# Small float32 units for short expert tails in a one-core attention and expert kernel

## The chip, the cores and the metric

The kernel runs on one core of one Trainium2 chip. The metric is device time in microseconds of one execution: 991.23 us is the median of three runs of the kernel before (988.27 to 992.65). Times inside an execution are in us from the first instruction of the profiled one.

## The reference, cut to what matters

Three stages follow each other: windowed attention over 4 x 768 tokens, a mixture of experts in which each token goes to one expert, and a dense layer with a rational activation. The change touches the second.

```python
N, D, E, F = (3072, 512, 8, 1024)
logits = x @ w_gate + modality_bias[modality_id]
e_idx = np.argmax(logits, axis=1)
...
for e in range(E):
    mask = e_idx == e
    if not mask.any():
        continue
    h = np.maximum(x[mask] @ w1[e], 0.0)
    out[mask] = gate_w[mask, None] * (h @ w2[e])
```

## The kernel before, in words

Attention works through 24 tiles of 128 tokens and writes each tile's output x to a buffer xd in HBM. `Router` then counts the tokens of each expert and cuts every expert's list into units of 128 tokens: the expert that is most frequent in the first 16 tiles comes first, the others follow by index, and the last unit of each expert may be partly empty. `second` (line 521) holds this arithmetic as a list of small VectorE operations that are issued by hand between TensorE's first products: the number of units of each expert (c), where each expert's units begin (off) and end (end), and each token's slot (slot, from T, lines 548 to 565). From the slots follow, by products with one-hot matrices, the token numbers of each unit (src_u, line 589), their places in the output buffer yd (pos_u) and the gate values (gate_s). `slots` (line 637) writes three flags per unit: is its expert another than that of the unit before, which expert is it, and is the unit used.

`Experts` does the units. `gather` (line 709) fetches the x of a unit by an indirect DMA that GpSimd (POOL) issues, into one of three buffers xg. `prep_x` (line 812) transposes it on TensorE and splits it into a high and a low float32r part. `mm1` (line 823) is three products, in 24 matmuls of 512 columns: x high and x low with w1 high, x high with w1 low. `relu` follows on ScalarE, `prep_h` (line 746) transposes and splits h in two halves, `mm2` (line 755) has again 24 matmuls, and `out` (line 765) scales by the gate on ScalarE and scatters the rows to yd by an indirect DMA from POOL. The raw weights of an expert, 2 MB for w1 and 2 MB for w2, are fetched by `load_w` (line 725) in four DMAs on SyncE's (SP's) queue, and split by `split_w` (line 738) on ScalarE and VectorE, both only where the flag says that the expert changes. SP, ScalarE and VectorE each read the flags and branch.

`moe` (line 841) is the order of the work, written out by hand: iteration i issues mm1 of unit i with the two halves of prep_h of unit i - 1 in between, then relu of unit i, prep_x of unit i + 1, and mm2 of unit i - 1. The weights w1 of unit i + 2 are fetched at the end of iteration i, those of w2 of unit i in its middle. Units 0 to 2 are partly done in `second`, units 3 to 25 in this loop, always; units 26 to 30 lie behind a branch that is taken only if the flag of unit 26 says so. Every engine runs its instructions in this order, and TensorE never goes past an instruction that waits.

`filler` is one step of `converter` (line 958), which turns the int64-coded weights of the third stage into float32r pairs: one DMA into the double buffer wr on SP, casts on ScalarE, five operations on VectorE. The loop calls it twice in an iteration while i < 12 and once after that.

Of the kernel before, what the change touches and what calls it, by code (L numbers as in the profile page):

```python
# [15 lines left out]
U32 = mybir.dt.uint32  # L16
# [266 lines left out]
        rt.second()  # L283


NS = 31
D_M = 512
BIGI = 4096.0
GP = 2048.0
# [3 lines left out]
class Router:  # L293
# [8 lines left out]
    def __init__(self, nc, rk, wk, tp, ident, logits, mod, mbias, pos_u, out_u, ex):  # L302
        self.pos_u, self.out_u, self.ex = pos_u, out_u, ex
        self.nc, self.wk, self.tp, self.ident, self.L = nc, wk, tp, ident, logits
        self.mod, self.mbias, self.src_u, self.flags = mod, mbias, ex.src_u, ex.flags

        def one(shape, dt, name):
            return rk.tile(shape, dt, name=name)

        self.iota = one([P, P], F16, "iota")  # L310
        self.tri = one([P, P], F16, "tri")
        self.ones = one([P, P], F16, "ones")
        self.w8 = one([P, E], F32, "w8")
# [10 lines left out]
        self.s = one([P, 6, E], F32, "s")  # L324
        self.k = one([P, 3], F32, "k")
        self.pidx = one([P, 1], F32, "pidx")
        one([P, 16], F32, "pad_k")
# [14 lines left out]
    def fixed(self):  # L342
        G = self.nc.gpsimd
        G.iota(self.i32, pattern=[[1, P]], base=0, channel_multiplier=0, allow_small_or_imprecise_dtypes=True)
        G.iota(self.w8, pattern=[[-1, E]], base=E, channel_multiplier=0, allow_small_or_imprecise_dtypes=True)

        G.iota(self.tok[:, 0:NT // 2], pattern=[[P, NT // 2]], base=-NT * P // 2, channel_multiplier=1, allow_small_or_imprecise_dtypes=True)
        G.iota(self.tok[:, NT // 2:], pattern=[[P, NT // 2]], base=1, channel_multiplier=1, allow_small_or_imprecise_dtypes=True)
        G.iota(self.pidx, pattern=[[0, 1]], base=0, channel_multiplier=1, allow_small_or_imprecise_dtypes=True)
# [171 lines left out]
    def second(self):  # L521
# [12 lines left out]
        rest = self.first_rest()  # L534
        for f in rest[:2]:
            f()
        c, end, off, hot, lt, other = [self.s[:, i] for i in range(6)]
        hi, slot = self.v[:, 3], self.v[:, 5]
        at2 = self.at2
        S3 = [P, 32, NT]  # L540
        be = self.wk.tile(S3, F16, tag="pt", name="be")
# [4 lines left out]
        for f in (  # L546
            p[0],
            lambda: V.tensor_scalar(out=c, in0=ps[:, NT - n], scalar1=1.0 / P, scalar2=127.0 / 256, op0=ALU.mult, op1=ALU.add),
            p[1],
            lambda: V.tensor_scalar(out=c, in0=c, scalar1=ROUND, scalar2=-ROUND, op0=ALU.add, op1=ALU.add),  # L550
            p[2],
            lambda: V.tensor_tensor_scan(out=end, data0=self.ones[:, 0:E], data1=c, initial=0.0, op0=ALU.mult, op1=ALU.add),
            p[3],
            lambda: V.tensor_tensor(out=hot, in0=hot, in1=c, op=ALU.mult),
            p[4],
            lambda: V.reduce_sum(self.k[:, 2:3], hot, axis=AX.X),
            lambda: V.tensor_tensor(out=off, in0=end, in1=c, op=ALU.subtract),
            lambda: V.scalar_tensor_tensor(out=off, in0=lt, scalar=self.k[:, 2:3], in1=off, op0=ALU.mult, op1=ALU.add),
            lambda: V.tensor_tensor(out=off, in0=off, in1=other, op=ALU.mult),
            lambda: V.tensor_tensor(out=self.T, in0=self.O, in1=off[:, None, :].to_broadcast([P, NT, E]), op=ALU.mult),  # L560
            lambda: V.reduce_sum(slot, self.T, axis=AX.X),
            lambda: V.tensor_tensor(out=s16, in0=slot, in1=hi, op=ALU.add),
            lambda: V.tensor_tensor(out=be, in0=s16[:, None, :].to_broadcast(S3), in1=self.ix, op=ALU.is_equal),
            lambda: V.tensor_tensor(out=bt, in0=be, in1=self.tok[:, None, :].to_broadcast(S3), op=ALU.mult),
            lambda: self.rows(at2, n, NT),
        ):
            f()
# [29 lines left out]
        self.slots(c, end, off, f, cnt)  # L597
        low = ex.prep_x(EARLY)
        ex.relu(1)
        ex.mm2_0(0, 0)  # L600
# [33 lines left out]
        ex.out(1, ex.ys1)  # L634
        ex.load_w(EARLY, ex.w2r, ex.w2v)

    def slots(self, c, end, off, f, cnt):

        V = self.nc.vector
        le = self.wk.tile([P, 32, E], F32, tag="pT", name="le")  # L640
        z, fl = f[:, 2], f[:, 3:6]
        S3 = [P, 32, E]
        V.tensor_tensor(out=end, in0=off, in1=c, op=ALU.add)
        V.tensor_tensor(out=le, in0=end[:, None, :].to_broadcast(S3), in1=self.iota[:, 0:32, None].to_broadcast(S3), op=ALU.is_gt)
        le2 = self.wk.tile([P, 32, E], F32, tag="pT", name="le2")
        V.tensor_tensor(out=le2, in0=off[:, None, :].to_broadcast(S3), in1=self.iota[:, 0:32, None].to_broadcast(S3), op=ALU.is_le)
        V.tensor_tensor(out=le, in0=le, in1=le2, op=ALU.mult)
        V.tensor_tensor(out=le, in0=le, in1=self.w8[:, None, :].to_broadcast(S3), op=ALU.mult)
        V.reduce_sum(z, le, axis=AX.X)
        V.tensor_scalar(out=fl[:, 2, :], in0=z, scalar1=0.0, scalar2=None, op0=ALU.is_gt)  # L650
        V.tensor_scalar(out=fl[:, 1, :], in0=z, scalar1=-1.0, scalar2=float(E), op0=ALU.mult, op1=ALU.add)
        V.tensor_scalar_min(fl[:, 1, :], fl[:, 1, :], float(E - 1))
# [11 lines left out]
class Experts:  # L664


    def __init__(self, nc, tc, ident, xd, yd, w1, w2, src_u, pos_u, out_u, gate_s):
        self.nc, self.tc, self.ident = nc, tc, ident
        self.xd, self.yd, self.src_u, self.pos_u, self.out_u, self.gate_s = xd, yd, src_u, pos_u, out_u, gate_s
        self.w1v = w1.rearrange("e (p k) f -> (e p) (k f)", k=4)  # L670
        self.w2v = w2.rearrange("e (p j) d -> (e p) (j d)", j=8)
        self.hps, self.yps, self.hT = {}, {}, {}
        self.ctx = ExitStack()
        self.sp = self.ctx.enter_context(tc.tile_pool(name="shared", side="right", bufs=1))
# [50 lines left out]
    def load_w(self, s, raw, view):  # L725
        nc = self.nc
        ch = nc.sync.value_load(self.flags[0:1, 0, s:s + 1], min_val=0, max_val=1)
        e = nc.sync.value_load(self.flags[0:1, 1, s:s + 1], min_val=0, max_val=E - 1)
        with self.tc.If(ch == 1):
            self.load(e, raw, view)  # L730

    def split_hi(self, raw, hi, i):
        self.nc.scalar.copy(hi[:, i], raw[:, i])  # L733
# [71 lines left out]
    def relu(self, s):  # L805
        ps = self.hps.pop(s)
        for i in range(2):
            self.nc.scalar.activation(
                self.hs[:, :, i * 64:(i + 1) * 64].rearrange("p j q -> p q j"), ps[i].rearrange("p (q j) -> p q j", j=8), func=AF.Relu,
            )  # L810
# [24 lines left out]
                )  # L835


NM = NT + 2


def moe(nc, tc, ex, filler, rows):
# [2 lines left out]
    w1r, w1h, w1l, w2r, w1v, w2v = ex.w1r, ex.w1h, ex.w1l, ex.w2r, ex.w1v, ex.w2v  # L844
    w2h, w2l = ex.w2h, ex.w2l
    gather, load_w, split_w, mm1, relu, prep_h, mm2, out = ex.gather, ex.load_w, ex.split_w, ex.mm1, ex.relu, ex.prep_h, ex.mm2, ex.out
    for i in range(EARLY + 1, NM + 1):
# [27 lines left out]
        if i == NM:  # L875
            for t in range(4):
                ps = ex.ps.tile([P, 4, P], F32, tag="t", name="yps") if t < 2 else ex.pb[t - 2].rearrange("p (k n) -> p k n", k=4)
                rows.prep(t, w1r[:, t, 0:D_M + 1], ps, rows.h, rows.l)

        if i + 1 < NM:  # L880
            split_w(i + 1, w1r, w1h, w1l)
        if i + 2 < NM:
            load_w(i + 2, w1r, w1v)
        if i == NM:
            ALL = (ET.PE, ET.Activation, ET.DVE, ET.Pool)
# [1 line left out]
            tc.mark_branch_hint_location("more", "LikelyTaken", engines=(ET.PE,))  # L887
        for part in range(2):
            mm2(i - 1, part)
        filler()  # L890
        out(i - 1)
    with tc.If(more == 1, label="more"):  # L892
        for i in range(NM, NS):
            load_w(i, w1r, w1v)
            load_w(i, w2r, w2v)
            split_w(i, w1r, w1h, w1l)
# [357 lines left out]
```

## Time and profile before

| | |
|---|---|
| time of the profiled execution | 991.19 us |
| its span, first to last instruction | 989.4 us |
| TensorE (PE) busy | 958.0 us, 97% |
| VectorE (DVE) busy | 749.6 us, 76% |
| ScalarE (ACT) busy | 594.6 us, 60% |
| GpSimd (POOL) busy | 146.5 us, 15% |
| attention, about | 0 to 107 us |
| router and experts, about | 107 to 447 us |
| third stage, about | 447 to 984 us |

A busy time is the time in which an engine had an instruction in flight. In a timeline a row is a run of instructions of the same kind: its start, how long it took, the engine, the line, what is written and read, the number of instructions, and in brackets the idle time just before it with what ended it. PE's records overlap: the next one starts before the last has ended, so the distance between starts is the price of a row. A plain float32 product leaves two records, a float32r product one. For a DMA, the time to landing runs from its issue to the arrival of its last byte.

### The profile page before, as it was taken

The page shows a single profiled execution, that of the slowest core. Times are in us where ns is not written, and L with a number is a line of the kernel's source. Part 1 is how long each engine was busy: PE and PEld are TensorE (multiplying, and loading weights), DVE is VectorE, ACT ScalarE, POOL GpSimd, SP SyncE. Part 2 cuts the span into 40 slices and gives each one's busy share as a digit, 9 for nine tenths or more (in the row PEclk, how much of TensorE's full clock was granted, in tenths as well). Part 3 has the DMA queues.
Part 4 walks back from the last instruction along what each step waited for, and adds up shares of the span by engine and source line. Part 5 has one row for each costly group of instructions (what it writes and reads, how often), then busy time and mean ns, then how long its engine had stood idle before and what let it go on. Part 6 is the DMA issues. An engine that isn't in the chain of part 4 may idle for free.

```text
span 989.4 us, 16219 instructions
## 1 busy us (share of the span) xinstructions
PE 958.0 (97%) x5825; PEld 780.5 (79%) x5825; DVE 749.6 (76%) x1220; ACT 594.6 (60%) x947; POOL 146.5 (15%) x205
## 2 busy tenths in 40 slices
PE   4998999999899999999999999999999999999997
PEld 3776678888778888887888888888888888888885
DVE  5777664666675553347999989988998998999885
ACT  2554534555575654456777766766676676767673
POOL 5111112111133333220000100100010001001001
PEclk9999999999999999999999999999999999999999
DMA  8999522443686654347120100100010000001001
GB/s 258 364 387 355 201 76 81 128 129 110 230 306 221 232 149 129 124 152 288 34 85 11 43 22 23 43 1 21 23 43 11 22 23 32 21 1 43 1 1 42
DMA packets 37991, 110.41 MB, mean 112 GB/s; under 512 B 6950, under 2 KB 6978, under 8 KB 37892
## 3 DMA queue, kind: packets, MB, share of 16 engines
q1 hardware_dynamic: 27540, 76.43, 23.1%
q0 software_dynamic: 10352, 32.79, 9.3%
q8 instruction: 46, 0.75, 0.3%
q14 instruction: 53, 0.43, 0.1%
HBM read 82.44 MB, written 27.80 MB: 111 GB/s over the span
## 4 chain that ended last, share of the span: by engine, by line
PE 52%; DVE 1%; DMA 1%; ACT 0%; issue 0%; POOLq 0%; SPq 0%; POOL 0%; DVEq 0%
PE a L1126 9%; PE a L1124 9%; PE a L1125 9%; PE h L1067 8%; PE h L1069 8%; PE h L1068 8%; PE yps L952 1%; DMA wo<-wod 1%; DVE gl L1109 0%; DVE u L1099 0%; DVE q L1086 0%; DVE q L1098 0%; DVE q L1097 0%; DVE u L1087 0%; POOLq L1250 0%
## 5 line engine op out<-in xcount | busy, mean ns | idle before, releaser
L1067 PE MATMUL h<-yh,wih 128*128 128x512 f32 x384 | 151.7, 395 | 0.4 <-PEq L892 0.4
L1126 PE MATMUL a<-wo,gl 128*128 128x512 f32 x384 | 149.7, 390 | 1.3 <-DVE gl L1109 1.3
L1124 PE MATMUL a<-wo,gh 128*128 128x512 f32 x384 | 149.5, 389 | 0.7 <-ACT gh L1103 0.7
L1068 PE MATMUL h<-yl,wih 128*128 128x512 f32 x384 | 149.6, 390 | 0.0
L1069 PE MATMUL h<-yh,wil 128*128 128x512 f32 x384 | 149.6, 390 | 0.0
L1125 PE MATMUL a<-wo,gh 128*128 128x512 f32 x384 | 149.4, 389 | 0.0
L832 PE MATMUL pb<-w1h,xs 128*128 128x512 f32 x400 | 104.2, 403 | 2.7 <-ACT w1h L733 2.7
L1079 ACT ACTIVATE s<-h 128x512 f32<-128x512 f32 x96 | 56.6, 590 | 80.2 <-PE h L1069 80.2
L1086 DVE SCALAR_TENSOR_TENSOR q<-s,ab,q 128x512 f32<-128x512 f32 x96 | 71.7, 747 | 27.5 <-ACT q L1080 27.5
L832 PEld LDWEIGHTS pb<-w1h,xs 128*128 128x128 f32 x400 | 74.1, 191 | 18.7 <-ACT w1h L733 3.2
L1103 ACT CAST gh<-u 128x512 fp32r<-128x512 f32 x96 | 59.9, 624 | 46.2 <-DVE u L1099 46.2
L1126 PEld LDWEIGHTS a<-wo,gl 128*128 128x128 f32 x384 | 72.1, 188 | 17.0 <-DVE gl L1109 2.1
L1124 PEld LDWEIGHTS a<-wo,gh 128*128 128x128 f32 x384 | 72.1, 188 | 16.1 <-ACT gh L1103 1.3
L1069 PEld LDWEIGHTS h<-yh,wil 128*128 128x128 f32 x384 | 72.1, 188 | 15.5
L1067 PEld LDWEIGHTS h<-yh,wih 128*128 128x128 f32 x384 | 72.1, 188 | 15.3 <-issue 0.8
L1125 PEld LDWEIGHTS a<-wo,gh 128*128 128x128 f32 x384 | 72.1, 188 | 14.9
L1068 PEld LDWEIGHTS h<-yl,wih 128*128 128x128 f32 x384 | 72.2, 188 | 14.4
L1081 ACT ACTIVATE u<-h,ab 128x512 f32<-128x512 f32 x96 | 74.9, 780 | 0.0
L1099 DVE SCALAR_TENSOR_TENSOR u<-u,ab,q 128x512 f32<-128x512 f32 x96 | 72.2, 752 | 3.4
L1088 DVE SCALAR_TENSOR_TENSOR u<-u,ab,h 128x512 f32<-128x512 f32 x96 | 71.8, 748 | 3.4
L753 DVE TENSOR_TENSOR hl<-hTp,hh 128x512 fp32r<-128x512 f32 x50 | 34.1, 688 | 50.6 <-ACT hh L752 50.4
L1097 DVE SCALAR_TENSOR_TENSOR q<-q,ab,s 128x512 f32<-128x512 f32 x96 | 71.7, 747 | 0.1
(225 smaller groups left out, 1754.1 us busy)
## 6 DMA issues: line engine op xcount, KB each, us to landing
v<-in_v SPq DMA_DIRECT2D x48, 260.0 KB, 5.4
w1r<-in_moe_w SPq DMA_DIRECT2D x16, 512.0 KB, 6.7
w2r<-in_moe_w SPq DMA_DIRECT2D x16, 512.0 KB, 8.7
wr<-in_moe_w_in SPq DMA_DIRECT2D x16, 512.0 KB, 3.7
wr<-in_moe_w_out SPq DMA_DIRECT2D x16, 512.0 KB, 4.4
wod<-wo POOLq DMA_DIRECT2D x32, 256.0 KB, 4.6
wo<-wod SPq DMA_DIRECT2D x16, 512.0 KB, 8.4
k<-in_k SPq DMA_DIRECT2D x48, 168.0 KB, 5.2
```

The source lines that it names most:

```text
L832: self.nc.tensor.matmul(ps[i], lhsT=x[:, kk, :], rhs=w[:, kk, i * 512:(i + 1) * 512], start=(x is h and w is w1h and kk == 0), stop=(w is ...
L1067: nc.tensor.matmul(ps, lhsT=wih[k][:, sl], rhs=h[:, k], start=(k == 0), stop=False)
L1068: nc.tensor.matmul(ps, lhsT=wih[k][:, sl], rhs=l[:, k], start=False, stop=False)
L1069: nc.tensor.matmul(ps, lhsT=wil[k][:, sl], rhs=h[:, k], start=False, stop=(k == NK - 1))
L1081: A.activation(u, ps, func=AF.Identity, scale=a3, bias=a2)
L1086: V.scalar_tensor_tensor(out=q, in0=s, scalar=absb1, in1=q, op0=ALU.mult, op1=ALU.add)
L1088: V.scalar_tensor_tensor(out=u, in0=u, scalar=a1, in1=ps, op0=ALU.add, op1=ALU.mult)
L1097: V.scalar_tensor_tensor(out=q, in0=q, scalar=cb, in1=s, op0=ALU.add, op1=ALU.mult)
L1099: V.scalar_tensor_tensor(out=u, in0=u, scalar=a0, in1=q, op0=ALU.add, op1=ALU.mult)
L1124: nc.tensor.matmul(ps, lhsT=gh[:, sl], rhs=wo[x][:, 0].bitcast(F32R), start=(x == 0), stop=False)
L1125: nc.tensor.matmul(ps, lhsT=gh[:, sl], rhs=wo[x][:, 1].bitcast(F32R), start=False, stop=False)
L1126: nc.tensor.matmul(ps, lhsT=gl[:, sl], rhs=wo[x][:, 0].bitcast(F32R), start=False, stop=(x == NF - 1))
```

## The change

Up to two experts whose last, partly filled unit holds at most 32 tokens lose that unit; a small unit takes its tokens instead. The router finds such tails (sm), takes them out of the count c, and gives the first of them slot 31 and the second slot 30. The static loop has 24 units (NM = NT) and not 26. The first small unit is done in iterations 5 and 6, the second in iterations 7 and 8.

A small unit uses the raw float32 weights, in the buffers w1r and w2r, without any split. Its w1 is fetched at the end of the iteration before, its w2 in the middle of its first iteration, both without a condition. Its 32 rows are gathered into the buffer of the unit whose x has just been used, which also holds its transposed x, its h and its transposed h. mm1_small makes 16 float32 matmuls with 32 stationary columns each; the four that follow each other write four different groups of 32 partitions of one bank of PSUM. mm2_small makes 32 of them in the same way. The gathers of units 8 and 10 move from the start of iterations 6 and 8 to behind the small unit's output. The double calls of filler last while i < 14.

```diff
-NS = 31
+NS = 32
+NN = 31
+SMALL = 2
+SM = 32
...
+            lambda: V.scalar_tensor_tensor(out=sm, in0=c, scalar=float(P), in1=ps[:, NT - n], op0=ALU.mult, op1=ALU.subtract),
+            p[3],
+            lambda: V.tensor_scalar(out=sm, in0=sm, scalar1=float(P - SM), scalar2=None, op0=ALU.is_ge),
+            p[4],
+            lambda: V.tensor_tensor_scan(out=cum, data0=self.ones[:, 0:E], data1=sm, initial=0.0, op0=ALU.mult, op1=ALU.add),
+            lambda: V.scalar_tensor_tensor(out=sm, in0=cum, scalar=float(SMALL), in1=sm, op0=ALU.is_le, op1=ALU.mult),
+            lambda: V.tensor_tensor(out=c, in0=c, in1=sm, op=ALU.subtract),
+            lambda: V.scalar_tensor_tensor(out=col, in0=cum, scalar=float(NS), in1=sm, op0=ALU.subtract, op1=ALU.mult),
...
-            lambda: V.tensor_tensor(out=self.T, in0=self.O, in1=off[:, None, :].to_broadcast([P, NT, E]), op=ALU.mult),
+            lambda: V.tensor_tensor(out=end, in0=off, in1=c, op=ALU.add),
+            lambda: V.scalar_tensor_tensor(out=by, in0=col, scalar=-1.0, in1=end, op0=ALU.mult, op1=ALU.subtract),
+            lambda: V.tensor_tensor(out=self.T, in0=hi[:, :, None].to_broadcast(ST), in1=c[:, None, :].to_broadcast(ST), op=ALU.is_ge),
+            lambda: V.tensor_tensor(out=self.T, in0=self.T, in1=by[:, None, :].to_broadcast(ST), op=ALU.mult),
+            lambda: V.tensor_tensor(out=self.T, in0=self.T, in1=off[:, None, :].to_broadcast(ST), op=ALU.add),
+            lambda: V.tensor_tensor(out=self.T, in0=self.T, in1=self.O, op=ALU.mult),
...
-        V.tensor_tensor(out=end, in0=off, in1=c, op=ALU.add)
...
+        V.tensor_tensor(out=ls, in0=col[:, None, :].to_broadcast(SS), in1=self.nid[:, :, None].to_broadcast(SS), op=ALU.is_equal)
+        V.tensor_tensor(out=ls, in0=ls, in1=self.w8[:, None, :].to_broadcast(SS), op=ALU.mult)
...
+        V.reduce_sum(zs, ls, axis=AX.X)
+        V.tensor_tensor(out=z[:, NS - SMALL:NS], in0=z[:, NS - SMALL:NS], in1=zs, op=ALU.add)
...
+    def load_small(self, k, raw, second):
+        nc, s = self.nc, NS - 1 - k
+        e = nc.sync.value_load(self.flags[0:1, 1, s:s + 1], min_val=0, max_val=E - 1)
+        if second:
+            v = self.w2n[bass.ds(e, 1)].rearrange("e (n p) d -> p (e n) d", p=P)
+            raw = raw.rearrange("p a (b d) -> p (a b) d", d=D_M)
+            for i in range(4):
+                nc.sync.dma_start(out=raw[:, 2 * i:2 * i + 2], in_=v[:, 2 * i:2 * i + 2])
+        else:
+            self.load(e, raw, self.w1v)
...
+    def prep_x_small(self, x, xT):
+
+        ps = self.ps.tile([P, 4, P], F32, tag="t", name="xps")
+        for kk in range(4):
+            self.nc.tensor.transpose(ps[:, kk, 0:SM], x[0:SM, kk:D_M:4], self.ident[0:SM, 0:SM])
+        self.nc.scalar.copy(xT, ps[:, :, 0:SM])
+
+    def mm1_small(self, xT, h):
+
+        ps = self.ps.tile([P, 256], F32, tag="t", name="sps")
+        for kk in range(4):
+            for c in range(4):
+                self.nc.tensor.matmul(
+                    ps[SM * c:SM * c + SM], lhsT=xT[:, kk, :], rhs=self.w1r[:, kk, 256 * c:256 * c + 256], start=(kk == 0), stop=(kk == 3),
+                )
+        self.nc.scalar.activation(h, ps, func=AF.Relu)
...
+    def mm2_small(self, hT):
+        ps = self.ps.tile([P, P], F32, tag="t", name="syp")
+        w = self.w2r.rearrange("p a (b d) -> p (a b) d", d=D_M)
+        for n in range(8):
+            for c in range(4):
+                self.nc.tensor.matmul(
+                    ps[SM * c:SM * c + SM], lhsT=hT[:, n % 2, SM * (n // 2):SM * (n // 2) + SM], rhs=w[:, n, P * c:P * c + P],
+                    start=(n == 0), stop=(n == 7),
+                )
+        return ps
...
-NM = NT + 2
+NM = NT
+FIRST_SMALL = {5: 0, 7: 1}
...
+        now, then = FIRST_SMALL.get(i), FIRST_SMALL.get(i - 1)
         if i < NM:
-            if i + 2 < NM:
+            if i + 2 < NM and then is None:
                 gather(i + 2)
+            if now is not None:
+                sx = ex.xg[i % 3]
+                sT = sx[:, 384:512].rearrange("p (k n) -> p k n", k=4)
+                ex.gather_small(now, sx)
             for part in range(3):
                 mm1(i, part)
                 if part < 2:
                     prep_h(i - 1, part)
+            if then is not None:
+                y = ex.mm2_small(small.pop(then))
+                ex.out_small(then, y)
+                if i + 2 < NM:
+                    gather(i + 2)
+                load_w(i - 1, w2r, w2v)
             split_w(i - 1, w2r, w2h, w2l)
             relu(i)
+            if now is not None:
+                ex.prep_x_small(sx, sT)
             if i + 1 < NM:
                 ex.prep_x(i + 1)()
...
-        if i < 12:
+        if i < 14:
             filler()
-        if i < NM:
+        if now is not None:
+            ex.load_small(now, w2r, True)
+        elif i < NM:
             load_w(i, w2r, w2v)
...
+        if now is not None:
+            ex.mm1_small(sT, sx[:, 0:256])
+            load_w(i + 1, w1r, w1v)
         if i + 1 < NM:
             split_w(i + 1, w1r, w1h, w1l)
-        if i + 2 < NM:
+        if i + 1 in FIRST_SMALL:
+            ex.load_small(FIRST_SMALL[i + 1], w1r, False)
+        elif i + 2 < NM:
             load_w(i + 2, w1r, w1v)
...
         for part in range(2):
             mm2(i - 1, part)
+            if now is not None and part == 0:
+                small[now] = sx[:, 256:512].rearrange("p (i n) -> p i n", i=2)
+                ex.prep_h_small(sx[:, 0:256], small[now])
```

Beside these, `gather_small` is an indirect DMA of 32 rows from POOL, `prep_h_small` two transposes on TensorE and a copy on ScalarE, and `out_small` one small copy on POOL, four activations of 32 partitions and 128 columns on ScalarE, and an indirect DMA of 32 rows from POOL.

## Rows read from the trace of the kernel before

**Rows 1.** The page, part 1: busy time, share of the span, instructions.
```profile
PE 958.0 (97%) x5825; PEld 780.5 (79%) x5825; DVE 749.6 (76%) x1220; ACT 594.6 (60%) x947; POOL 146.5 (15%) x205
```

**Rows 2.** Busy time by stretch: length, busy us of each engine, PE's clock, DMA.
```profile
175.00:200.00 25.00, 25.00 (x123) 20.80 (x122) 15.47 (x27) 13.05 (x20) 4.83 (x6) 1.00 0.43 128
```

**Rows 3.** Timeline of PE, starts of mm1 and of prep_x, units 4 to 6.
```profile
161.29 1.98 PE L832 MATMUL pb<-w1h,xs 128*128 128x512 f32 x8
...
173.65 1.98 PE L832 MATMUL pb<-w1h,xs 128*128 128x512 f32 x8
...
180.06 0.63 PE L817 MATMUL xps<-ident,xg 128*128 128x128 f32 x4
...
186.00 1.98 PE L832 MATMUL pb<-w1h,xs 128*128 128x512 f32 x8
```

**Rows 4.** Timeline of PE, starts of mm1 around two changes of expert.
```profile
247.76 1.98 PE L832 MATMUL pb<-w1h,xs 128*128 128x512 f32 x8
...
263.03 3.58 PE L832 MATMUL pb<-w1h,xs 128*128 128x512 f32 x8 [2.75 <-ACT w1h L733]
...
277.02 1.98 PE L832 MATMUL pb<-w1h,xs 128*128 128x512 f32 x8
...
303.52 1.98 PE L832 MATMUL pb<-w1h,xs 128*128 128x512 f32 x8
```

**Rows 5.** Timeline of ACT, steps of the converter.
```profile
173.77 0.65 ACT L984 CAST wih<-wr 128x512 fp32r<-128x512 f32 x1 [2.49 <-DVE wr L930]
...
247.90 0.65 ACT L984 CAST wih<-wr 128x512 fp32r<-128x512 f32 x1 [2.49 <-DVE wr L930]
...
261.27 0.66 ACT L926 ACTIVATE wf<-wr 128x512 f32<-128x512 f32 x1 [4.09 <-DMA wr<-in_moe_w_out]
```

**Rows 6.** Timeline of PE in attention: float32 products on four column groups.
```profile
95.83 1.07 PE L200 MATMUL gps<-xT,wg 128*32 128x512 f32 x8
...
97.41 1.09 PE L169 MATMUL pv<-v,pT 128*32 128x130 f32 x32
```

**Rows 7.** Timeline of POOL: issues of gathers.
```profile
123.08 1.20 POOL L711 DMA_INDIRECT xg<-xd,src_u  x1 [20.02 <-DVE s L643]
...
178.89 1.04 POOL L711 DMA_INDIRECT xg<-xd,src_u  x1 [0.30 <-issue]
...
252.91 1.04 POOL L711 DMA_INDIRECT xg<-xd,src_u  x1 [0.30 <-issue]
...
283.62 1.06 POOL L711 DMA_INDIRECT xg<-xd,src_u  x1 [0.30 <-PE pb L832]
```

**Rows 8.** Timeline of SP's queue: the load of w1 for unit 12.
```profile
249.22 2.36 SPq L718 DMA_DIRECT2D w1r<-in_moe_w  x4
```

**Rows 9.** DMA issues of the whole span: count, median us to landing.
```profile
xg<-xd,src_u POOLq DMA_INDIRECT x26, 3.8
```

**Rows 10.** DMA issues from 250 to 258 us.
```profile
xg<-xd,src_u POOLq DMA_INDIRECT x1, 8.1
```

**Rows 11.** A stretch: length, POOL busy, PE's clock, DMA share, GB/s.
```profile
263.00:263.50 0.50, 0.00 (x0) 0.50 0.00 0
```

**Rows 12.** Timeline of DVE in the router.
```profile
113.70 0.17 DVE L430 TENSOR_SCALAR route<-route 128x8 f32<-128x8 f32 x1
...
114.92 0.36 DVE L560 TENSOR_TENSOR T<-O,s 128x192 f32<-128x192 f16 x1
...
126.82 0.22 DVE L659 TENSOR_TENSOR_SCAN f<-ones,cnt 128x32 f32<-128x32 f16 x1 [0.87 <-PE cnt L596]
```

**Rows 13.** DMA issues from 122 to 128 us.
```profile
xg<-xd,src_u POOLq DMA_INDIRECT x3, 3.6
```

**Rows 14.** Timeline of PE: transposes of unit 2's x.
```profile
126.80 0.72 PE L817 MATMUL xps<-ident,xg 128*128 128x128 f32 x4
```

**Rows 15.** DMA issues from 272 to 280 us: count, KB each, us to landing.
```profile
w2r<-in_moe_w SPq DMA_DIRECT2D x4, 512.0 KB, 8.6
```

**Rows 16.** DMA issues from 280 to 290 us.
```profile
xg<-xd,src_u POOLq DMA_INDIRECT x1, 3.8
```

More of the change, by code (lines that the diff above doesn't have):

```diff
@@ L323, in __init__ @@
         self.v = one([P, 6, NT], F32, "route")
-        self.s = one([P, 6, E], F32, "s")
+        self.s = one([P, 10, E], F32, "s")
         self.k = one([P, 3], F32, "k")
         self.pidx = one([P, 1], F32, "pidx")
+        self.nid = one([P, SMALL], F32, "nid")
         one([P, 16], F32, "pad_k")
@@ L348, in fixed @@
         G.iota(self.tok[:, NT // 2:], pattern=[[P, NT // 2]], base=1, channel_multiplier=1, allow_small_or_imprecise_dtypes=True)
+        G.iota(self.nid, pattern=[[-1, SMALL]], base=SMALL - NS, channel_multiplier=0, allow_small_or_imprecise_dtypes=True)
         G.iota(self.pidx, pattern=[[0, 1]], base=0, channel_multiplier=1, allow_small_or_imprecise_dtypes=True)
@@ L536, in second @@
             f()
-        c, end, off, hot, lt, other = [self.s[:, i] for i in range(6)]
+        c, end, off, hot, lt, other, sm, cum, col, by = [self.s[:, i] for i in range(10)]
         hi, slot = self.v[:, 3], self.v[:, 5]
+        ST = [P, NT, E]
         at2 = self.at2
@@ L551, in second @@
             p[2],
+            lambda: V.scalar_tensor_tensor(out=sm, in0=c, scalar=float(P), in1=ps[:, NT - n], op0=ALU.mult, op1=ALU.subtract),
[6 more added lines that the diff above has]
+            lambda: V.scalar_tensor_tensor(out=col, in0=cum, scalar=float(NS), in1=sm, op0=ALU.subtract, op1=ALU.mult),
             lambda: V.tensor_tensor_scan(out=end, data0=self.ones[:, 0:E], data1=c, initial=0.0, op0=ALU.mult, op1=ALU.add),
-            p[3],
             lambda: V.tensor_tensor(out=hot, in0=hot, in1=c, op=ALU.mult),
-            p[4],
             lambda: V.reduce_sum(self.k[:, 2:3], hot, axis=AX.X),
@@ L596, in second @@
         nc.tensor.matmul(cnt, lhsT=self.ones, rhs=some, start=True, stop=True)
-        self.slots(c, end, off, f, cnt)
+        self.slots(col, end, off, f, cnt)
         low = ex.prep_x(EARLY)
@@ L635, in second, with slots @@
         ex.load_w(EARLY, ex.w2r, ex.w2v)
-    def slots(self, c, end, off, f, cnt):
+    def slots(self, col, end, off, f, cnt):
         V = self.nc.vector
@@ L649, in slots @@
         V.reduce_sum(z, le, axis=AX.X)
+        SS = [P, SMALL, E]
+        ls = self.wk.tile(SS, F32, tag="mx", name="ls")
+        V.tensor_tensor(out=ls, in0=col[:, None, :].to_broadcast(SS), in1=self.nid[:, :, None].to_broadcast(SS), op=ALU.is_equal)
+        V.tensor_tensor(out=ls, in0=ls, in1=self.w8[:, None, :].to_broadcast(SS), op=ALU.mult)
+        zs = self.wk.tile([P, SMALL], F32, tag="rs", name="zs")
+        V.reduce_sum(zs, ls, axis=AX.X)
+        V.tensor_tensor(out=z[:, NS - SMALL:NS], in0=z[:, NS - SMALL:NS], in1=zs, op=ALU.add)
         V.tensor_scalar(out=fl[:, 2, :], in0=z, scalar1=0.0, scalar2=None, op0=ALU.is_gt)
@@ L671, in __init__ @@
         self.w2v = w2.rearrange("e (p j) d -> (e p) (j d)", j=8)
+        self.w2n = w2
         self.hps, self.yps, self.hT = {}, {}, {}
@@ new lines, in gather_small @@
+    def gather_small(self, k, x):
+        s, rows = NS - 1 - k, row(NT)
+        self.nc.gpsimd.indirect_dma_start(
+            out=x[0:SM], out_offset=None, in_=self.xd[0:rows], in_offset=bass.IndirectOffsetOnAxis(ap=self.src_u[0:SM, s:s + 1], axis=0),
+            bounds_check=rows - 1, oob_is_err=False,
+        )
[4 more added lines that the diff above has]
+        self.nc.scalar.copy(xT, ps[:, :, 0:SM])
@@ new lines, in mm1_small, with prep_h_small @@
+    def mm1_small(self, xT, h):
[6 more added lines that the diff above has]
+        self.nc.scalar.activation(h, ps, func=AF.Relu)
+    def prep_h_small(self, h, hT):
+        ps = self.ps.tile([P, 2, P], F32, tag="t", name="shp")
+        for i in range(2):
+            self.nc.tensor.transpose(ps[:, i, :], h[:, i * P:(i + 1) * P], self.ident)
+        self.nc.scalar.copy(hT, ps)
@@ new lines, in mm2_small, with out_small @@
+    def mm2_small(self, hT):
[6 more added lines that the diff above has]
+                    start=(n == 0), stop=(n == 7),
+                )
+        return ps
+    def out_small(self, k, ps):
+        nc, y, s = self.nc, self.ys, NS - 1 - k
+        nc.gpsimd.tensor_copy(y[0:SM, D_M:].bitcast(U32), self.out_u[0:SM, s:s + 1])
+        for c in range(4):
+            nc.scalar.activation(y[0:SM, P * c:P * c + P], ps[SM * c:SM * c + SM], func=AF.Copy, scale=self.gate_s[0:SM, s:s + 1])
+        nc.gpsimd.indirect_dma_start(
+            out=self.yd, out_offset=bass.IndirectOffsetOnAxis(ap=self.pos_u[0:SM, s:s + 1], axis=0), in_=y[0:SM], in_offset=None,
+            bounds_check=NT * P - 1, oob_is_err=False,
+        )
@@ L846, in moe @@
     gather, load_w, split_w, mm1, relu, prep_h, mm2, out = ex.gather, ex.load_w, ex.split_w, ex.mm1, ex.relu, ex.prep_h, ex.mm2, ex.out
+    small = {}
     for i in range(EARLY + 1, NM + 1):
+        now, then = FIRST_SMALL.get(i), FIRST_SMALL.get(i - 1)
         if i < NM:
-            if i + 2 < NM:
+            if i + 2 < NM and then is None:
                 gather(i + 2)
+            if now is not None:
+                sx = ex.xg[i % 3]
+                sT = sx[:, 384:512].rearrange("p (k n) -> p k n", k=4)
+                ex.gather_small(now, sx)
             for part in range(3):
@@ L892, in moe @@
     with tc.If(more == 1, label="more"):
-        for i in range(NM, NS):
+        for i in range(NM, NN):
             load_w(i, w1r, w1v)
```

## The prediction, made blind

> **What bounds the kernel now.** I read the page first: TensorE (PE) is busy for 958.0 of 989.4 us [rows 1], so the time is nearly the sum of what PE is given, plus the places where it stands still. The table by stretches says the same of the expert stage, which the change touches: 25.00 of 25 us busy, at a granted clock of 1.00, while ScalarE (ACT) and VectorE (DVE) have room [rows 2]. The timeline of PE gives the price of a unit of 128 tokens: mm1 of units 4, 5 and 6 starts at 161.29, 173.65 and 186.00, so a unit is 12.35 us; in it, from the start of mm1 to the transposes of the next unit's x it is 6.41 us, and from there to the next mm1 5.94 us [rows 3]. The only idle time of note in the stage is where the expert changes [rows 4].
>
> Counting the reference's own routing for its inputs gives 1428, 494, 1145 and 5 tokens for experts 7, 2, 5 and 0, and none for the rest: 12 + 4 + 9 + 1 = 26 units. The tails of expert 7 (20) and of expert 0 (all its 5 tokens) are at most 32, so both become small units and 24 full ones are left. The branch behind `more` stays empty, so the change does what it says; other counts would make it fall through to that branch.
>
> **The change, part by part. Removed:** two full units, 2 x 12.35 = **-24.7 us**, and one of two changes of expert that follow on each other (7 to 0 to 2 becomes 7 to 2). From 247.76 to 303.52 four units take 55.76 us, where 49.40 is due, so the pair costs 6.36. The first change alone costs 277.02 - 247.76 - 24.70 = 4.56, then comes its split of w2, which I put at 0.8, between nothing and the 1.8 that are left. I keep 5.4 for the single change and take **-1.0** (0 to -1.8) [rows 4]. Its idle 2.75 us stays: ACT waits there, 4.09 us until 261.27, for a converter load (wr) queued behind the expert's 2 MB [rows 5], and as the filler's limit moves from 12 to 14, the change at unit 11 has the same two filler calls around it as the change at unit 12 has now.
>
> **PE work of a small unit.** Rows of attention have the same form, float32 on four column groups: 4 products of 512 columns (8 records) in 1.07 us, and 16 of 130 columns (32 records) in 1.09 us [rows 6]. So 16 products of 256 columns are 16 x 1.07/8 = 2.1 us and 32 of 128 columns 2.2 us. The six transposes are at most 6 x 0.63/4 = 0.9 us [rows 3]; four of them have 32 columns, so I take 0.5. Together 4.8, for two units **+9.6** (8.6 to 10.4). If the groups did not overlap, a product would cost four times as much; the rows exclude that for single products, not for sums of them.
> PE goes from 128-column products to 32-column ones and back without an idle time in these rows: from 95.83 to 98.50 the records of the two groups and of the four transposes between them add up to 1.07 + 0.63 + 1.09 = 2.79 us in 2.67 [rows 3, 6]. So I price these changes at nothing.
> The Trainium skill (TensorEngine Tiling (Array Packing), Tiling Modes) says that a change of tiling mode drains TensorE, which speaks against small units between full ones. By that each of six changes in a unit would lose such an overlap, 0.06 us by those rows, and the sum would be 0.7 us longer.
>
> **The wait for the small gather.** This term decides. `prep_x_small` stands on PE behind mm1 of unit 5 and ahead of everything else, so PE cannot go on to the next transposes, nor to mm2 of unit 4, until 32 gathered rows have landed. They are gathered in the same iteration: POOL first scatters unit 3, gathers unit 7 at 178.89, and can issue the small gather some 1.3 us later, at 180.2 [rows 7]. mm1 of unit 5 ends at 180.06 [rows 3]. So PE waits whatever the transfer takes.
> In the median of all 26 a gather lands 3.8 us after issue [rows 9], which gives 184.0 and a wait of 3.9 us. But at the end of iteration 4 `load_small` puts 2 MB of w1 on SP's queue, where before nothing was loaded. Its place is that of the load at 249.22 for unit 12: that one was issued 1.32 us after the second converter cast on ACT at 247.90, and the cast of iteration 4 is at 173.77, so the load starts at 175.1 [rows 5, 8]. Beside that load the gather issued at 252.91 took 8.1 us, to 261.0, which is 11.8 us after the load began [rows 7, 10]. The same distance gives 175.1 + 11.8 = 186.9, a wait of **6.8 us**.
> For the second one let U be the end of mm1 of unit 6. mm2_small (2.2) goes in there, so mm1 of unit 7 ends at U + 2.2 + 5.94 + 6.41 = U + 14.55. On ACT the four evacuations of the small unit (at 0.25 each) come before relu, so the load starts not 7.4 us after the end of mm1, as in the case above (175.1 less 180.06 - 12.35), but 2.2 + 1.0 later, at U + 10.6; it lands, with the gather, at U + 22.4: **7.8 us**. Both **+14.6**; with 3.8 us to land it would be 3.9 + 5.1 = 9.0 (the second is issued 1.2 us later against mm1, as ACT scales unit 5 later by as much), and with the small gather queued a whole gather (1.3 us) behind, 17.2. I take the value of the case with a load beside it, since that is what the change puts there.
>
> **The clock.** After the idle 2.75 us PE ran at 0.50 of its clock, 1.2 GHz, and the eight products that followed took 3.58 us instead of 1.98 [rows 4, 11]. A wait of 7 us will do so too: 2 x 1.6 = **+3.2** (0 to 4).
>
> **The router's chain on DVE.** Before the sum that yields each token's slot, the change adds eight operations on 8 columns and three on 192. Ten small ones take 1.22 us from 113.70 to 114.92, where two chains interleave; the added ones mostly follow on each other, so 8 x 0.18 = 1.4, and 3 x 0.4 = 1.2 (the one there now takes 0.36) [rows 12]. This is on the path: DVE's src_u releases the gather of unit 2 at 123.08, which lands 3.6 us later, at 126.7, and PE starts on its x at 126.80 [rows 7, 13, 14]. **+2.6** (0 if a cover appears, 4.2 if the idle time halves the clock). Of the new steps in `slots`, all after src_u, four small ones (0.7 us) lie in the 0.87 us for which DVE waits for cnt anyway [rows 12]; without that idle time they would delay the split of w2 by as much.
>
> **Costed at nothing.** Relu and copies of the small unit on ACT: mm2's first half, 2.7 us, hides them, if ACT is not held by a converter load; the one behind the small w1 lands with the gather. The delayed gathers of units 8 and 10 have a whole iteration. The four w2 pieces: SP issues them some 4.3 us after the small gather is there (transposes, two copies, the converter's cast and load come first), and mm2_small comes 17 us after it (4.2 of small work and slow clock, 5.5 of mm2, 6.5 of mm1, and the rest). A w2 piece next to other traffic lands 8.6 us after issue [rows 15], and four are issued within 2.4 us at best [rows 8], so they are there at 15.3 or a little later: just in time. The two SP value loads per skipped `load_w` were there before; the iota on POOL lies in the load phase.
>
> Sum: -24.7 - 1.0 + 9.6 + 14.6 + 3.2 + 2.6 = **+4.3 us** on the profiled execution's 991.2, which is also the median of the runs (991.23): **995.5 us**, 0.4% above. A measurement of this kernel can tell about 0.5% from no change, that is 986.3 to 996.2, so I forecast no change to speak of: two units go, and two waits give it back.
>
> **Rivals.** (1) *The small gather lands quickly*: 32 rows of 2 KB get through beside the load. Waits of 9.0 instead of 14.6 us give 990; with the router's additions hidden or no fall of the clock, 987. For: a gather at 283.62, with w2 in flight, took only 3.8 us [rows 7, 16]. Against: the 8.1 us above, with a load that had just begun [rows 10].
> The Trainium skill (DMA: Bandwidth & Descriptors, Queues, rings and completion order) says that each DMA engine takes packets of its queues in turn. By that the short gather would share and land early, at 990 us; the 8.1 us beside the load do not look so, but they are of 128 rows.
> (2) *Slower: w2 comes late.* The w2 of a small unit is fetched in rows of 2 KB instead of 4 KB, and if the four pieces take over 12.7 us, mm2_small, in front of the next transposes, waits. At 2 us of wait and 1.6 of slow clock in each unit that is +7.2: 1002.7. Twice 8.6 us for a piece would put the last at 4.3 + 2.4 + 17.2 = 23.9, 6.9 us late, and the time at 1012.
> (3) *Sums on column groups do not overlap*: the products cost (2.1 + 2.2) x 3 more per unit, +26: 1021.
>
> **How the numbers follow.** The forecast has 0.48 (990 to 1001; of it 0.02 faster, 0.26 same, 0.20 slower), rival 1 0.28 (983 to 994; half faster, half same), rival 2 0.18, rival 3 and anything like a spill into the spare branch 0.06. Faster 0.16, same 0.40, slower 0.44. The range goes from rival 1's better half to rival 2, 984 to 1005; the likeliest case's own is 990 to 1001.
>
> **What would show it.** Right: 48 rows of mm1 and mm2 fewer per removed unit; two idle times of PE of 6 to 8 us before the transposes of `prep_x_small`, ended by the DMA into xg, with the clock at 0.5 after each; small products at about 70 ns each (128 columns); the second gather of iterations 5 and 7 taking over 6 us; the first PE stop near 120 us. Wrong: small transposes waiting under 5 us (rival 1), a wait on w2r ahead of mm2_small (rival 2), small products four times as long (rival 3).

## The result, and the profile after

The changed kernel takes 999.47 us in the median of five runs (997.2 to 1002.57), the kernel before 990.5 us in five (986.42 to 992.65): the ratio is 1.010, with a 95% interval of 1.0065 to 1.0135. It is slower by about 9 us, or 1%. The profiled executions differ by less, 998.14 against 991.19 us, in spans 996.3 against 989.4: the one of after lies 1.3 us below its median, that of before 0.7 above its own. The sums below are of the profiled executions and so explain 6.9 us.

The page, part 1, of the changed kernel (busy time, share of the span, instructions), to be read against [rows 1]:

```profile
PE 944.5 (95%) x5909; PEld 765.7 (77%) x5909; DVE 738.7 (74%) x1220; ACT 583.3 (59%) x941; POOL 144.2 (14%) x206
```

PE is busy for 13.5 us less and takes 6.9 us longer, so some 20 us more of standing still have come in. The waits of PE from 100 to 460 us name them (line, what it waited for, us in total, times, longest; ACTq is ScalarE's sequencer, which takes its branches):

```profile
PE xps L778 <- DMA xg<-xd,src_u: 12.9, 2, 6.5
PE pb L918 <- ACT w1h L819: 2.6, 1, 2.6
PE pa L846 <- ACTq L827: 2.0, 2, 1.0
PE pa L846 <- DVE hl L839: 1.4, 1, 1.4
PE xps L903 <- DVE out_u L681: 1.3, 1, 1.3
PE pa L846 <- ACT w2h L819: 1.2, 1, 1.2
PE pb L918 <- ACTq L827: 0.9, 1, 0.9
```

L918 is the old L832, and its wait for w1h is about as long as it was, 2.6 for 2.75 us [rows 4]. The wait for w2h was 0.4 us in all before. The others are new. The longest, L778, is `prep_x_small`. The timeline of PE shows where they lie; unit 3's mm1 starts at 149.85, unit 5's at 174.55, unit 7's at 213.52, unit 9's at 253.46:

```profile
149.85 1.98 PE L918 MATMUL pb<-w1h,xs 128*128 128x512 f32 x8
...
174.55 1.98 PE L918 MATMUL pb<-w1h,xs 128*128 128x512 f32 x8
...
187.57 0.66 PE L778 MATMUL xps<-ident,xg 32*128 32x32 f32 x4 [6.45 <-DMA xg<-xd,src_u]
188.16 1.13 PE L903 MATMUL xps<-ident,xg 128*128 128x128 f32 x4
189.22 2.80 PE L786 MATMUL sps<-w1r,xg 128*32 128x256 f32 x32
191.94 1.20 PE L846 MATMUL pa<-w2h,hh 128*128 128x512 f32 x4
...
204.27 1.95 PE L802 MATMUL syp<-w2r,xg 128*32 128x128 f32 x64
...
207.93 1.20 PE L846 MATMUL pa<-w2h,hh 128*128 128x512 f32 x4 [1.02 <-ACTq L827]
...
213.52 1.98 PE L918 MATMUL pb<-w1h,xs 128*128 128x512 f32 x8
...
226.57 0.69 PE L778 MATMUL xps<-ident,xg 32*128 32x32 f32 x4 [6.48 <-DMA xg<-xd,src_u]
...
253.46 1.98 PE L918 MATMUL pb<-w1h,xs 128*128 128x512 f32 x8
```

Two full units are 24.70 us [rows 3]. With a small unit among them two take 38.97 (174.55 to 213.52) and 39.94 us: a small unit costs 14.3 and 15.2 us where a full one costs 12.35. The clock after the wait (length, busy us of PE, PE's load, DVE, ACT and POOL, then PE's clock, DMA share and GB/s):

```profile
186.00:192.00 6.00, 4.43 (x41) 2.55 (x41) 2.02 (x4) 2.02 (x4) 0.18 (x1) 0.58 0.04 12
```

PE's clock is at 0.58 in the mean of this stretch, so nearly all of it ran at 0.50, which is 1.2 GHz. And the change of expert, four units from mm1 of unit 10 to mm1 of unit 14, which answers to [rows 4]:

```profile
265.81 1.98 PE L918 MATMUL pb<-w1h,xs 128*128 128x512 f32 x8
...
280.89 2.14 PE L918 MATMUL pb<-w1h,xs 128*128 128x512 f32 x8 [2.57 <-ACT w1h L819]
...
290.42 1.21 PE L846 MATMUL pa<-w2h,hl 128*128 128x512 f32 x4 [1.39 <-DVE hl L839]
...
307.02 0.74 PE L846 MATMUL pa<-w2h,hh 128*128 128x512 f32 x2 [1.22 <-ACT w2h L819]
...
310.56 2.11 PE L918 MATMUL pb<-w1h,xs 128*128 128x512 f32 x8 [0.94 <-ACTq L827]
...
323.08 1.98 PE L918 MATMUL pb<-w1h,xs 128*128 128x512 f32 x8
```

These take 57.27 us, where 49.40 is due: one change of expert costs 7.87, more than the pair of before with its 6.36.

The sum of the profiled executions: up to mm1 of unit 3 it is 149.85 against 148.94, +0.9; the stretch with the small units 103.61, six full units of 74.10 and 29.5 on top; two full units less, -24.7; the change of expert +1.5; the rest, up to the end, -0.3. Together +6.9.

### The profile page after: what moved, and what is told of

The parts are those of the page before. It is cut to its first block, busy times and chain, and to the rows that moved or that the text cites. A ratio compares the mean times of both kernels' runs of the same rounds, so it can differ in the third digit from the quotient of the medians.

```text
span 996.3 us, 16316 instructions
## 1 busy us (share of the span) xinstructions
PE 944.5 (95%) x5909; PEld 765.7 (77%) x5909; DVE 738.7 (74%) x1220; ACT 583.3 (59%) x941; POOL 144.2 (14%) x206
## 4 chain that ended last, share of the span: by engine, by line
PE 51%; DVE 1%; DMA 1%; ACT 0%; issue 0%; POOLq 0%; SPq 0%; POOL 0%
PE a L1237 9%; PE a L1235 9%; PE a L1236 8%; PE h L1178 8%; PE h L1180 8%; PE h L1179 8%; PE yps L1063 1%; DMA wo<-wod 1%; DMA yd<-ys,pos_u 0%; DVE gl L1220 0%; DVE u L1210 0%; DVE q L1197 0%; DVE q L1209 0%; DVE q L1208 0%; DVE u L1198 0%
## 5 line engine op out<-in xcount | busy, mean ns | idle before, releaser
L918 PE MATMUL pb<-w1h,xs 128*128 128x512 f32 x368 | 94.4, 399 | 3.5 <-ACT w1h L819 2.6
L918 PEld LDWEIGHTS pb<-w1h,xs 128*128 128x128 f32 x368 | 67.2, 188 | 18.1 <-ACT w1h L819 3.2
L1203 ACT ACTIVATE s<-q,ab 128x512 f32<-128x512 f32 x96 | 70.2, 731 | 1.2 <-DVE q L1197 0.2
```

The source lines that it names most:

```text
L918: self.nc.tensor.matmul(ps[i], lhsT=x[:, kk, :], rhs=w[:, kk, i * 512:(i + 1) * 512], start=(x is h and w is w1h and kk == 0), stop=(w is ...
```

## The experiments

**The small gather one iteration earlier.** If the wait for the gather is the loss, it goes when the gather is issued right after the transposes that free its buffer, before the load of w1 has begun.

```diff
-                ex.gather_small(now, sx)
...
                 ex.prep_x(i + 1)()
+            if i + 1 in FIRST_SMALL:
+                ex.gather_small(FIRST_SMALL[i + 1], ex.xg[(i + 1) % 3])
```

> Edit: each small gather is issued one iteration earlier, right after the transposes that free its buffer, ahead of the small unit's load of w1. Theory A (the loss is the wait for the small gather beside the load): both idle times of 6.5 us before the small transposes vanish, and so does the slow clock after them (2 x 1.6 us); in their place the small products wait some 1.5 us each for ScalarE's copy of the transposed x, which stands behind relu of the full unit. So 12.9 + 3.2 - 3.0 = 13 us less than the changed kernel: about 986 us, ratio to the kernel before 0.993 to 0.998. Rival B (the small units' own products and changes between the array's modes are the loss, and the wait only lies beside them): the idle time moves to the next instruction and the time falls by under 4 us, to 995 or more.

Measured: 986.0 us (median of 10 runs), ratio to before 0.9971 (0.9953 to 0.9989). Timeline of PE:

```profile
175.74 1.98 PE L918 MATMUL pb<-w1h,xs 128*128 128x512 f32 x8
...
182.23 0.66 PE L778 MATMUL xps<-ident,xg 32*128 32x32 f32 x4
...
184.27 1.94 PE L786 MATMUL sps<-w1r,xg 128*32 128x256 f32 x32 [0.70 <-ACT xg L779]
...
207.72 1.98 PE L918 MATMUL pb<-w1h,xs 128*128 128x512 f32 x8
...
218.03 0.64 PE L786 MATMUL sps<-w1r,xg 128*32 128x256 f32 x8 [0.26 <-DMA w1r<-in_moe_w]
...
240.19 1.98 PE L918 MATMUL pb<-w1h,xs 128*128 128x512 f32 x8
```

The wait and the slow clock are gone; ScalarE's copy costs 0.70 us for each small unit, not the 1.5 that were expected. The two units now take 31.98 us (175.74 to 207.72) instead of 38.97, the next two 32.47 instead of 39.94; in these the small products also stop for the last part of w1, which without the long wait arrives only just in time. So 14.5 us of the small units' cost was the place of the gather, and moving the call turns a loss into a small gain, 0.3%. Rival B falls.

**Without the small units' load of w1.** What makes the gather slow, its neighbour on its own queue or the 2 MB beside it?

```diff
-            ex.load_small(FIRST_SMALL[i + 1], w1r, False)
+            pass
```

> Edit: the small units' two loads of w1 are left out, so their products use whatever w1 the buffer holds and 25 tokens come out otherwise; all else is as in the changed kernel. Theory A (the 2 MB load beside the gather makes it slow): the small gather lands within about 3 us of its issue instead of 6.4, and the two idle times fall from 6.5 to about 3 us each, not to zero, since the gather is still issued only when mm1 has ended; about 7 us less than the changed kernel. Rival C (an indirect DMA that follows another on its queue is slow by itself, whatever else moves): the idle times stay at 6.5 us.

Measured: one run, 992.18 us, too few to go by the time. The waits of PE:

```profile
PE xps L778 <- DMA xg<-xd,src_u: 6.3, 2, 3.4
```

The two waits fall from 12.9 to 6.3 us. In iteration 5 the full gather, issued at 180.10, and the small one behind it, issued at 181.44, land after 3.9 and 2.7 us (DMA issues of 180 to 181 and of 181.5 to 183 us):

```profile
xg<-xd,src_u POOLq DMA_INDIRECT x1, 3.9
...
xg<-xd,src_u POOLq DMA_INDIRECT x1, 2.7
```

The same two of the changed kernel, issued at 179.80 and 181.14 (DMA issues of 179 to 180 and of 181 to 183 us):

```profile
xg<-xd,src_u POOLq DMA_INDIRECT x1, 7.5
...
xg<-xd,src_u POOLq DMA_INDIRECT x1, 6.3
```

So half of the wait is the load that moves beside the gathers, and half is that the small gather is issued too late for any transfer. Rival C falls. One thing stays open: by these rows the small gather lands 0.1 us behind the full one both times, at 187.44 and 187.30 with the load, at 184.14 and 184.00 without it. No run issues it ahead of the full one beside the load, so whether it waits for the load itself or for the gather in front of it is not shown.

The pairs of units take 35.62 and 36.24 us here, 3.4 and 3.7 less than in the changed kernel; the waits are 3.5 and 3.1 shorter, so it is about the shorter wait and no more. So the price of the slow clock is still paid after idle times of 2.9 and 3.4 us; the granted clock is 0.50 from 185 to 188 and from 223 to 225 us.

**The double converter steps elsewhere.**

```diff
-        if i < 14:
+        if i < 10 or 18 <= i < 22:
```

> Edit: the second converter step of an iteration is taken in iterations 3 to 9 and 18 to 21 instead of 3 to 13; the number of steps is the same. Theory A (the double steps now lie on the split of w1 and w2 for unit 11): the stretch of four units around the change of expert, 57.3 us in the changed kernel, comes down to about 51, with the idle times of 2.6, 1.4, 1.2 and 0.9 us gone; the whole time falls by 4 to 6 us, to about 994. Rival: the splits themselves (8 casts and 8 subtractions of 1024 columns) are too long for the room that ScalarE and VectorE have, and the stretch stays above 55.

Measured: 990.19 us (10 runs), ratio to before 1.0014 (0.9996 to 1.0032). Timeline of PE, starts of mm1 of units 10 and 14:

```profile
264.36 1.98 PE L918 MATMUL pb<-w1h,xs 128*128 128x512 f32 x8
...
314.12 1.98 PE L918 MATMUL pb<-w1h,xs 128*128 128x512 f32 x8
```

The four units take 49.76 us, 0.36 above four plain ones, and none of the four idle times is left. The gain, 57.27 - 49.76 = 7.5 us, is larger than the 4 to 6 that were expected, as the splits are hidden entirely. The rival falls. As all second steps from iteration 10 to 13 moved at once, the run shows that they cause these waits, and not which step causes which.

**The small evacuation later.**

```diff
                 y = ex.mm2_small(small.pop(then))
-                ex.out_small(then, y)
-                if i + 2 < NM:
-                    gather(i + 2)
                 load_w(i - 1, w2r, w2v)
...
                 ex.prep_x(i + 1)()
+            if then is not None:
+                ex.out_small(then, y)
+                if i + 2 < NM:
+                    gather(i + 2)
```

> Edit: the small unit's evacuation, scatter and the gather behind it are issued after relu and after the transposes of the next unit, not right behind its products. Theory A (mm2 of the full unit waits 1.0 us because ScalarE takes its branch on the unchanged w2 only after the four small evacuations): both idle times of 1.0 us before mm2 in iterations 6 and 8 vanish, 2 us less in all, and nothing else moves. Rival (PE waits there for the transposes' own copies or for PSUM space): the idle times stay, or come back before the next mm1.

Measured: one run, 996.03 us, too few to go by the time. Timeline of PE in iteration 6:

```profile
203.45 1.95 PE L802 MATMUL syp<-w2r,xg 128*32 128x128 f32 x64
205.33 0.75 PE L903 MATMUL xps<-ident,xg 128*128 128x128 f32 x4
205.84 1.18 PE L846 MATMUL pa<-w2h,hh 128*128 128x512 f32 x4
```

mm2 of unit 5 follows the transposes without a stop; the 2.0 us of ACTq waits in front of mm2 are gone, and no new wait takes their place. What PE waited for was a branch, as L827 is the `If` of the split. The full unit's w2 may be split anew in that iteration, so mm2 has to know that ScalarE has passed the point where it would be, even where it skips the split; and ScalarE came to that point only behind four evacuations of the small unit.

**The router's additions alone**, in the kernel before.

```diff
+            lambda: V.scalar_tensor_tensor(out=sm, in0=c, scalar=float(P), in1=ps[:, NT - n], op0=ALU.mult, op1=ALU.subtract),
+            lambda: V.tensor_scalar(out=sm, in0=sm, scalar1=4096.0, scalar2=None, op0=ALU.is_ge),
...
-            lambda: V.tensor_tensor(out=self.T, in0=self.O, in1=off[:, None, :].to_broadcast([P, NT, E]), op=ALU.mult),
+            lambda: V.tensor_tensor(out=self.T, in0=hi[:, :, None].to_broadcast(ST), in1=c[:, None, :].to_broadcast(ST), op=ALU.is_ge),
...
```

> Edit: the kernel before, with the change's additions to the router's chain ahead of the slot sum alone (eight operations on 8 columns, three on 192; the threshold for a small tail is set so high that none is found, so the units stay as they were). Theory A (this chain is on TensorE's path): the transposes of unit 2 wait some 1.3 us and the slot products 0.6 us; the kernel is 2 to 2.6 us slower than before, ratio 1.002 to 1.003; where TensorE's clock rises earlier by chance in a run, up to 1.7 us of it can be hidden. Rival (the chain is covered, since the changed kernel's mm1 of unit 3 starts only 0.9 us later than before): under 1 us, ratio 1.000 to 1.001.

Measured: 991.09 us (12 runs), ratio 1.0012 (0.9997 to 1.0027): by the time alone it cannot be told from either expectation. The timeline of PE tells more:

```profile
110.47 3.44 PE L799 MATMUL pa<-w1r,x 128*128 128x512 f32 x4 [0.68 <-ACT x L792]
...
120.50 1.66 PE L592 MATMUL tb<-bt,at 128*128 128x32 f16 x24 [0.50 <-DVE bt L576]
...
130.09 0.72 PE L829 MATMUL xps<-ident,xg 128*128 128x128 f32 x4 [1.51 <-DVE pos_u L673]
...
152.30 1.98 PE L844 MATMUL pb<-w1h,xs 128*128 128x512 f32 x8
```

From the first product of unit 0 to mm1 of unit 3 it is 41.83 us, in the kernel before 148.94 - 109.19 = 39.75: 2.1 us, made of a wait of 0.50 before the slot products and one of 1.51 at the x of unit 2. In the changed kernel the same stretch, from 109.72 to 149.85, is 40.13 us, although it has the same two waits (0.60 and 1.28): there the first four records of that product took 1.98 us, here and before 3.4 to 3.7. From 110 to 112 us PE's granted clock is 1.00 in the changed kernel and 0.50 in the kernel before. This does not come from the change, since the last run below, with the router of before, has the short product too:

```profile
108.29 1.99 PE L787 MATMUL pa<-w1r,x 128*128 128x512 f32 x4 [0.68 <-ACT x L780]
...
146.24 1.98 PE L832 MATMUL pb<-w1h,xs 128*128 128x512 f32 x8
```

That is 37.95 us, and 40.13 less 37.95 gives 2.2 us for the router again. So the clock in this place is chance, 1.7 us of it, and it is why the profiled execution of after shows 0.9 us only. Of these 0.9, 0.5 lie ahead of the router (109.72 for 109.19).

**All of it together**, with the first half of mm2 put ahead of `mm1_small` as well, so that PE works while ScalarE copies the small x:

```diff
         if now is not None:
+            mm2(i - 1, 0)
             ex.mm1_small(sT, sx[:, 0:256])
             load_w(i + 1, w1r, w1v)
...
-        for part in range(2):
+        for part in range(0 if now is None else 1, 2):
             mm2(i - 1, part)
-            if now is not None and part == 0:
+            if now is not None:
```

> Edit: the early small gather, the late small evacuation and the moved converter steps of the other runs together, and the first half of mm2 put ahead of the small products of mm1, so that they do not wait for ScalarE's copy. Theory A (the losses are separate waits, and add up): from the span of 983.8 us with the early gather alone, 7.5 us go with the converter steps, 2.0 with the evacuation, 1.4 with the copy: span 973, time 975 us, ratio 0.983 to 0.987. Rival (the waits share a cause, VectorE and ScalarE being full, and come back elsewhere): 979 us or more.

Measured: 971.45 us (5 runs), ratio to before 0.9818 (0.9795 to 0.9842). It beats both kernels. Timeline of PE, iterations 5 and 6:

```profile
178.97 2.10 PE L918 MATMUL pb<-w1l,xs 128*128 128x512 f32 x8
181.00 0.66 PE L778 MATMUL xps<-ident,xg 32*128 32x32 f32 x4
181.59 0.75 PE L903 MATMUL xps<-ident,xg 128*128 128x128 f32 x4
182.10 1.17 PE L846 MATMUL pa<-w2h,hh 128*128 128x512 f32 x4
...
185.03 1.93 PE L786 MATMUL sps<-w1r,xg 128*32 128x256 f32 x32
186.89 1.20 PE L846 MATMUL pa<-w2h,hh 128*128 128x512 f32 x4
...
196.47 1.95 PE L802 MATMUL syp<-w2r,xg 128*32 128x128 f32 x64
198.36 0.75 PE L903 MATMUL xps<-ident,xg 128*128 128x128 f32 x4
...
204.42 1.98 PE L918 MATMUL pb<-w1h,xs 128*128 128x512 f32 x8
```

There is no idle time left in these iterations. mm1 of unit 5 starts at 174.51 here, so the two units take 29.91 us, and a small unit 5.2 where a full one takes 12.35. The time is 3.5 us better than expected: the pairs of units take 59.8 us and not 61.0; the change of expert takes 49.73 where the run with the early gather had 57.94, 8.2 less and not 7.5; and 1.2 us lie ahead of unit 3, where that run had the slow clock in the router and this one had not. The rival falls. All these runs have the routing of the same inputs.

**The moved converter steps in the kernel before.** How much of this belongs to the small units at all?

```diff
-        if i < 12:
+        if i < 10 or 18 <= i < 20:
```

> Edit: the kernel before, with its double converter steps in iterations 3 to 9 and 18 and 19 instead of 3 to 11. Theory A (what the moved steps save is the wait of the split of w1, and has nothing to do with small units): the idle 2.75 us at unit 12 and the slow clock after it vanish, 4 to 5 us less than before, ratio 0.995 to 0.996. Rival (with two changes of expert in a row the splits themselves fill ScalarE and VectorE): the stretch of four units stays within 1.5 us of its 55.8 us.

Measured: 983.53 us (4 runs), ratio 0.9936 (0.9913 to 0.9959). mm1 of unit 11 starts at 245.06, that of unit 15 at 295.09 (timeline of PE):

```profile
245.06 1.98 PE L832 MATMUL pb<-w1h,xs 128*128 128x512 f32 x8
...
295.09 1.98 PE L832 MATMUL pb<-w1h,xs 128*128 128x512 f32 x8
```

The four units take 50.03 us instead of 55.76, also with two changes of expert in a row. So of the 18 us between the kernel before (989.24 us beside these runs) and the best one, 5.7 are the converter's schedule, and 983.53 - 971.45 = 12.1 are the small units, to within some 3 us by the two intervals. That is what they should give: 24.7 for two units, less 2 x 5.2 for the small ones, less 2.1 for the router, 12.2.

## Why the prediction was right or wrong

The forecast was 995.5 us with a range from 984 to 1005, and its own case from 990 to 1001; 999.47 lies in both. It named no change to speak of, while its own chances had 0.40 on that and 0.44 on slower by over 0.5%; it is slower by 1.0%, so no change did not come true, and the interval leaves no room for it. The mechanism it put in the middle, two waits for the small gather that give back two units, is the one that the early gather and the run without the load show. Its numbers, term by term, for the profiled execution (forecast +4.3, measured +6.9):

- **Two units, -24.7:** so measured, 12.35 us each.
- **PE work of the small units, +9.6:** 10.4, from the best kernel. The products on column groups overlap as the rows of attention said, in sums too: the 16 of mm1 take 1.86 us (2.1 forecast), the 32 of mm2 1.89 (2.2). Rival 3 is out. The six transposes take 0.73 us for 0.5; the four of 32 columns alone take 0.59. The rest, which I had priced at nothing, is what a change between products of 128 and of 32 columns costs: from the start of mm1's last eight products to the small transposes it is 181.00 - 178.97 = 2.03 us, to ordinary transposes 180.06 - 178.11 = 1.95 in the kernel before. Over the six such places of a small unit the differences are 0.05 to 0.14 us and make 0.6. The reading was wrong and not only the size: rows at a change overlap by 0.06 us, but ordinary neighbours by more, 0.16 in the kernel before where the last products meet the transposes (178.11 + 2.11 - 180.06). The drain of which the Trainium skill tells (TensorEngine Tiling (Array Packing), Tiling Modes) agrees with these differences; no run shows the drain itself.
- **The wait, +14.6:** 12.9. The load began at 175.36, where the forecast's 175.1 with the 0.9 us of delay in front of it would be 176.0, and the small gather was there 12.1 us later (11.8 forecast): 6.45 us of wait for 6.8. The second wait, 6.48 for 7.8, was mis-sized on PE's side: from the end of unit 6's mm1 it is 15.8 us to the end of unit 7's, where I took 14.55, as PE stops for 1.0 us on the way (the last point here). Rival 1 did not come true: beside the load the small gathers took 6.3 and 6.0 us, without it 2.7 and 2.6. That DMA engines take packets of their queues in turn (the Trainium skill, DMA: Bandwidth & Descriptors, Queues, rings and completion order) did not let the short gather through quickly; as it stood behind a full one on its own queue, these runs do not test that rule for a short gather alone.
- **The clock, +3.2:** 4.1. It is what the pairs take beyond the best kernel's 29.91 us once the waits are off: 38.97 - 29.91 - 6.45 - 1.02 = 1.6, and 39.94 - 29.91 - 6.48 - 1.02 = 2.5. The products of mm1_small took 2.72 and 3.57 us instead of 1.86. The 1.6 of the forecast came from a single stop and was a little low.
- **The router, +2.6:** 2.1 by the run with it alone, of which 1.7 are hidden in the profiled execution by the clock, by luck.
- **The change of expert, -1.0:** +1.5, of the wrong sign. The step that failed is the sentence that the change at unit 11 has the same filler calls around it as the one at unit 12 had. That holds for the split of w1, one iteration before the unit, and its wait stayed (2.57 us). It does not hold for the unit's own iteration and the next, in which w2 is split: before, these were 12 and 13, with single converter steps; now they are 11 and 12, with double ones. In 11 VectorE was late for the split of h, in 12 ScalarE for the split of w2 and for the branch behind it: 1.39, 1.22 and 0.94 us. The run with the steps moved shows that the steps are the cause; that these three belong to the steps of 11 and 12 is argued from the rows.
- **Costed at nothing:** one wait was overlooked, 2.0 us in all, that of mm2 for ScalarE's branch behind the small evacuations. I had looked for who waits for the small unit's results, and not for what stands behind its evacuation on ScalarE. w2 arrived in time, so rival 2 is out.

So the sum fell 2.6 us short by two steps, the converter's calls (2.5) and ScalarE's order (2.0), with the small units' work and the slow clock 0.8 and 0.9 us over the forecast; the shorter waits (1.7), the router (0.5) and the clock in it (1.7, by luck) hid part of it. That the number came so near is in part this cancelling.

## What to carry to other kernels

Work that is cheap on an engine is not cheap if its input is fetched in the iteration that uses it: issue a gather when its buffer comes free, ahead of the large load, and put independent work between a short step and the copy on which the next step waits. When a loop gets shorter, look at every constant that was set against its length: here a limit moved up by two met a split that had moved down by one. A skipped branch is still an instruction in its engine's order, and whoever depends on what it might have done waits for it, here 1.0 us twice.

## What the runs showed that I had not expected

The kernel before had 5.7 us in the place of a few converter steps, and its two changes of expert in a row cost 0.6 us instead of 6.4 once ScalarE did not stand waiting for a converter's load ahead of the split (the 4.09 us of [rows 5] are not there in that run). And the small gather gained little by its size where it stood: issued 1.3 us behind a full one beside the load, 64 KB landed 6.3 us after issue, 0.1 us behind the 256 KB. Issued alone and ahead of the load, in the run with the early gather, it took 2.4 us.
